# Retention and two gated layers on one core: decays on values and queries, a second pair of score banks, weight conversion in small steps

## The chip, the cores and the metric

The kernel runs on one core of a Trainium2 chip. The metric is the device time of one execution in microseconds (us). Before the change it is 634.4 us, the median of three runs (631.55 to 635.45).

## What is computed

The first stage is retention, a recurrence per batch and head with a fixed decay gamma of the head; after it come two gated layers on its output.

```python
gamma = 1.0 - 2.0 ** (-5.0 - np.arange(H))
for t in range(S):
    state = gamma * state + k[t] (outer) v[t]      # per batch and head, 64 x 64
    y[t] = (1 / sqrt(D)) * q[t] @ state
x = y as (1536 tokens, 512)
x = ((x @ w_a) * (x @ w_b)) @ w_out                # d_ff 1536
h = x @ w_in;  out = (h * sigmoid(1.702 * h)) @ w_out2   # d_ff 2048
```

There are 2 batches, 8 heads, 768 time steps and 64 columns per head. The weights arrive as 64-bit floats and are turned on the chip into a high and a low float32 part, and every product of a layer is made as three matmuls of such parts.

## The kernel before

Retention is done in chunks. The 1536 tokens are 12 blocks of 128 (`NBLK`), six to a batch (`SEQ`). In block n, with c = n % 6:

- `att_load` brings q and k transposed and k and v plain into one tile `raw`, of which there are four. Load n+4 stands on SP's queue behind the last reader of block n.
- `att_scores` makes k'q for the 8 heads in two banks of PSUM, and VectorE multiplies them by `mask`, which holds causality, scale and gamma^(t-s) of every head (L144, two instructions). There is one pair of these banks, so scores of block n+1 wait until block n's masks are through.
- `att_kd` (GpSimd, L118) puts decays on k; `att_kv` adds kd'v to a bank that runs over the six blocks, and VectorE writes the state, scaled by `gdec` (L168, L170).
- `att_qd` (GpSimd, L109) puts decays on q; `att_av` makes v'a and, where c > 0, adds state'qd. ScalarE copies the sum to `xh` (L200), VectorE writes the rest, `xl` (L64).

A weight piece of 128x512 goes through three steps, each one `w_point` behind the other: `w_carry` (ScalarE, L234 and L235), `w_round` (four VectorE instructions, L242 to L249), and `w_parts` (ScalarE writes `wh` at L255, then GpSimd writes `wl` at L64). In retention there is one `w_point` at the end of blocks 3, 5, 7, 9 and 11. In the layers w_points stand behind every set of matmuls.

The schedule is manual: each engine runs its instructions in the order in which the program writes them. The layers, `up` (L296) and `down` (L333), come after block 11. The first `up` uses piece 0, the second piece 1, and so on.

Of the kernel before, what the change touches and what calls it, by code (L numbers as in the profile page):

```python
# [39 lines left out]
def retention_moe_kernel(  # L40
# [25 lines left out]

    mask = attp.tile([P, 2, NP, P], F32, tag="mask", name="mask", bufs=1)
    decays = attp.tile([P, NP * P + H + NP, 1], F32, tag="decays", name="decays", bufs=1)  # L70
    kdec = attp.tile([P, SEQ - 1, H, 1], F32, tag="kdec", name="kdec", bufs=1)
    kinv = attp.tile([P, SEQ - 1, H, 1], F32, tag="kinv", name="kinv", bufs=1)
    gdec = attp.tile([P, SEQ - 2, NP, 1], F32, tag="gdec", name="gdec", bufs=1)
    dec = decays[:, 0:NP * P].rearrange("p (a t) o -> p a (t o)", t=P)
    kdec0, gdec0 = decays[:, NP * P:NP * P + H], decays[:, NP * P + H:]
    zero = attp.tile([P, P], F32, tag="zero", name="zero", bufs=1)
    x = [xp.tile([P, KD, NT], F32R, tag=t, name=t) for t in ("xh", "xl")]
    raw_t, qd_t, kd_t, a_t, state_t = {}, {}, {}, {}, {}
    kv_t = [None]

    def att_load(n):
        if n >= NBLK:
            return
        t = attp.tile([P, 4, DM], F32, tag="raw", name="raw", bufs=RAWBUFS)
        if n == 0:
            m = cmask.rearrange("p (c h t) -> p c h t", c=2, t=P)
            nc.sync.dma_start(out=t[:, 0, :], in_=att[n][:, 0, :])
            nc.scalar.dma_start(out=t[:, 1, :], in_=att[n][:, 1, :])
            for h2 in range(2):
                nc.scalar.dma_start(out=mask[:, h2], in_=m[:, h2])  # L90
            nc.sync.dma_start(out=t[:, 2:4, :], in_=att[n][:, 2:4, :])
            nc.scalar.dma_start(out=decays.rearrange("p a o -> p (a o)"), in_=cdec)
        else:
            for i in (0, 2):
                nc.sync.dma_start(out=t[:, i:i + 2, :], in_=att[n][:, i:i + 2, :])
        raw_t[n] = t

    def att_decays():

        for c in range(1, SEQ - 1):  # L100
            nc.gpsimd.tensor_tensor(out=kdec[:, c], in0=kdec0, in1=kinv[:, c], op=ALU.mult)
        nc.gpsimd.tensor_copy(gdec[:, 0], gdec0)
        for c in range(1, SEQ - 2):
            nc.gpsimd.tensor_tensor(out=gdec[:, c], in0=gdec[:, c - 1], in1=gdec0, op=ALU.mult)

    def att_qd(n):
        if n < NBLK and n % SEQ > 0:
            t = attp.tile([P, NP, P], F32, tag="qd", name="qd")
            nc.gpsimd.tensor_tensor(  # L109
                out=t, in0=raw_t[n][:, 0, :].rearrange("p (a t) -> p a t", t=P), in1=dec, op=ALU.mult  # L110
            )
            qd_t[n] = t

    def att_kd(n):
        c = n % SEQ
        if n < NBLK and c < SEQ - 1:
            t = attp.tile([P, H, D], F32, tag="kd", name="kd")
            nc.gpsimd.tensor_tensor(  # L118
                out=t,
                in0=raw_t[n][:, 2, :].rearrange("p (h d) -> p h d", d=D),  # L120
                in1=(kdec[:, c] if c else kdec0).to_broadcast([P, H, D]),
                op=ALU.mult,
            )
            kd_t[n] = t

    def att_scores(n):

        if n >= NBLK:
            return
        r = raw_t[n]  # L130
        ps = [ps_att.tile([P, NP, P], F32, tag="sc", name="ps_sc", bufs=2) for _ in range(2)]
        for p in range(NP):
            for h2 in range(2):
                rows = slice(64 * h2, 64 * h2 + 64)
                nc.tensor.matmul(  # L135
                    ps[h2][:, p, :],
                    r[rows, 1, p * P:(p + 1) * P],
                    r[rows, 0, p * P:(p + 1) * P],
                    start=True,
                    stop=True,  # L140
                )
        for h2 in range(2):
            a = attp.tile([P, NP, P], F32, tag="a", name="a", bufs=4)
            nc.vector.tensor_tensor(out=a, in0=ps[h2], in1=mask[:, h2], op=ALU.mult)  # L144
            a_t[n, h2] = a

    def att_kv(n):
        c = n % SEQ
        if c == SEQ - 1:
            return  # L150
        if c == 0:
            kv_t[0] = ps_att.tile([P, NP, D], F32, tag="kv", name="ps_kv")
        ps = kv_t[0]
# [12 lines left out]
        t = attp.tile([P, NP, D], F32, tag="state", name="state")
        if c == 0:
            nc.vector.tensor_copy(t, ps)  # L168
        else:
            nc.vector.tensor_tensor(out=t, in0=ps, in1=gdec[:, c - 1].to_broadcast([P, NP, D]), op=ALU.mult)  # L170
        state_t[n + 1] = t

    def att_av(n):
        c = n % SEQ
        ps = ps_att.tile([P, NP, P], F32, tag="av", name="ps_av", bufs=2)
        for p in range(NP):
            for h2 in range(2):
                h = 2 * p + h2
                nc.tensor.matmul(  # L179
                    ps[64 * h2:64 * h2 + 64, p, :],  # L180
                    raw_t[n][:, 3, h * D:(h + 1) * D],
                    a_t[n, h2][:, p, :],
                    start=(p == 0),
                    stop=(c == 0),
                    skip_group_check=True,
                )
        if c > 0:
            for p in range(NP):
                for h2 in range(2):
                    rows = slice(64 * h2, 64 * h2 + 64)  # L190
                    nc.tensor.matmul(  # L191
                        ps[rows, p, :],
                        state_t[n][rows, p, :],
                        qd_t[n][rows, p, :],
                        start=False,
                        stop=True,
                        skip_group_check=True,
                    )
        hi, lo = (t[:, :, n * P:(n + 1) * P] for t in x)
        nc.scalar.copy(hi, ps)  # L200
        lo_part(nc.vector, lo, ps, hi)

# [31 lines left out]
        nc.scalar.activation(out=wt[i], in_=high.bitcast(F32), func=ACTF.Abs)  # L234
        nc.scalar.activation(out=low, in_=low.bitcast(U32), func=ACTF.Copy, scale=2.0 ** -29)  # L235

    def w_round(i):
        src = wraw.pop(i)
        carry, high = src[:, :, 0], src[:, :, 1]
        t = wt[i]  # L240
        ti = t.bitcast(I32)
        nc.vector.tensor_scalar(out=t, in0=t, scalar1=F64_LOW, scalar2=F64_HIGH, op0=ALU.max, op1=ALU.min)  # L242
        nc.vector.tensor_scalar(  # L243
            out=ti, in0=ti, scalar1=3, scalar2=0x3FFFFFFF, op0=ALU.logical_shift_left, op1=ALU.bitwise_and
        )
# [12 lines left out]
    def w_point():  # L258
# [117 lines left out]
    def layer(ph):  # L376
        nfb = (C1 if ph == 1 else C2) // FB
        for fb in range(nfb):
# [25 lines left out]
            for q in range(4):  # L404
# [5 lines left out]
                flush(ps, ph, fb, q, fine)  # L410
                w_points(2)

    with tc.manual_schedule():
        nc.vector.memset(zero, 0.0)
        for n in range(2):
            att_load(n)
        gamma = [1.0 - 2.0 ** (-5.0 - h) for h in range(H)]
        for c in range(1, SEQ - 1):
            for h in range(H):
                nc.gpsimd.memset(kinv[:, c, h, :], gamma[h] ** (-float(P) * c))  # L420

        ps = ps_att.tile([P, NP, P], F32, tag="av", name="ps_warm", bufs=2)
        for _ in range(WARM):
            nc.tensor.matmul(ps[:, 0, :], zero, zero, start=True, stop=True)
        att_load(2)
        att_load(3)
        att_scores(0)
        att_kd(0)
        att_decays()
        for n in range(NBLK):  # L430
            if n == 0:
                att_kv(n)
                att_scores(n + 1)
            else:
                att_scores(n + 1)
                att_kv(n)
            att_kd(n + 1)
            att_av(n)
            att_qd(n + 1)
            att_load(n + RAWBUFS)  # L440
            if n in (1, 2, 3):
# [71 lines left out]
```

## Time and profile before

| quantity | value |
|---|---|
| median of 3 runs | 634.4 us |
| time of the profiled execution | 635.11 us |
| span of the profiled execution (first to last instruction) | 633.2 us |
| mean granted TensorE clock | 0.976 of full |
| TensorE, VectorE, ScalarE, GpSimd busy | 611.5, 381.9, 227.7, 143.6 us |

The span is 1.9 us shorter than the time of the same execution. Busy shares are means over two stages: retention, some 72 us, and the layers after it. Line numbers are those of the kernel before. PE is TensorE's matmuls, DVE is VectorE, ACT ScalarE, POOL GpSimd, SP the engine that issues most transfers.

### The profile page before, as it was taken

What the parts mean: (1) busy time and instruction counts of PE and PEld (TensorE: products, weight loads), DVE (VectorE), ACT (ScalarE), POOL (GpSimd) and SP (SyncE); (2) the same over time, 40 slices, a digit from 0 to 9 for tenths busy, and PEclk for the clock granted to TensorE, in tenths of its full rate; (3) what the DMA queues carried; (4) which work ended last, traced back from release to release, by engine and by line L of the source; (5) the groups of instructions that cost most, each with busy time, mean ns of one, the idle gap of its engine ahead of it and who ended that gap; (6) DMA issues with size and microseconds to landing.
All of it is one profiled execution on the core that took longest, in us unless ns stands there. A gap on an engine that the chain in (4) does not pass through costs nothing.

```text
span 633.2 us, 7760 instructions
## 1 busy us (share of the span) xinstructions
PE 611.5 (97%) x3174; PEld 508.3 (80%) x3174; DVE 381.9 (60%) x433; ACT 227.7 (36%) x310; POOL 143.6 (23%) x132
## 2 busy tenths in 40 slices
PE   5977899999999999999999999999999999999996
PEld 5866688888888888888888888888888888888885
DVE  1667747786026878226886758762779277936422
ACT  0212245445124453014554245643554055314300
POOL 3534223333002332002331302230223021302000
PEclk7977799999999999999999999999999999999999
DMA  8883123333012222111222211140023112200022
GB/s 315 277 330 128 48 85 101 100 99 100 0 35 67 92 86 90 33 34 47 87 101 67 67 33 42 58 134 33 34 68 119 49 33 67 66 1 0 1 99 100
DMA packets 15491, 52.67 MB, mean 83 GB/s; under 512 B 1632, under 2 KB 1632, under 8 KB 15456
## 3 DMA queue, kind: packets, MB, share of 16 engines
q1 hardware_dynamic: 14880, 51.12, 24.2%
q10 hardware_dynamic: 576, 1.05, 0.5%
q8 instruction: 25, 0.41, 0.2%
q14 instruction: 10, 0.08, 0.0%
HBM read 49.03 MB, written 3.15 MB: 82 GB/s over the span
## 4 chain that ended last, share of the span: by engine, by line
PE 93%; DVE 3%; DMA 2%; ACTq 0%; ACT 0%; POOL 0%; issue 0%; DVEq 0%; SPq 0%; POOLq 0%
PE ps L296 52%; PE ps L333 36%; PE ps_sc L135 2%; PE ps_av L179 2%; DMA decays<-in_cdec_dram 1%; PE ps_av L191 1%; DMA raw<-in_att_dram 1%; PE ps_kv L158 1%; DVE wt L246 1%; DVE wt L242 0%; DVE wt L249 0%; DVE wt L243 0%; DVE a L144 0%; DVE xl L64 0%; DVE part L350 0%; ACT xh L200 0%
## 5 line engine op out<-in xcount | busy, mean ns | idle before, releaser
L64 POOL TENSOR_TENSOR wl<-wt,wh 128x512 fp32r<-128x512 f32 x68 | 116.6, 1718 | 421.1 <-ACT wh L255 396.4
L296 PE MATMUL ps<-xh,wh 128*128 128x512 f32 x480 | 129.7, 391 | 0.0
L296 PE MATMUL ps<-xl,wh 128*128 128x512 f32 x480 | 128.8, 389 | 0.0
L296 PE MATMUL ps<-xh,wl 128*128 128x512 f32 x480 | 128.8, 389 | 0.0
L296 PEld LDWEIGHTS ps<-xh,wh 128*128 128x128 f32 x480 | 90.5, 189 | 19.1 <-issue 0.3
L296 PEld LDWEIGHTS ps<-xl,wh 128*128 128x128 f32 x480 | 90.2, 188 | 18.8
L296 PEld LDWEIGHTS ps<-xh,wl 128*128 128x128 f32 x480 | 90.1, 188 | 18.7
L242 DVE TENSOR_SCALAR wt<-wt 128x512 f32<-128x512 f32 x68 | 67.0, 986 | 55.6 <-ACT wt L234 55.6
L313 ACT CAST gh<-sb 128x1536 fp32r<-128x1536 f32 (+1 forms) x42 | 44.2, 1051 | 111.6 <-DVE sb L312 111.6
L64 DVE TENSOR_TENSOR gl<-sb,gh 128x1536 fp32r<-128x1536 f32 (+1 forms) x42 | 51.5, 1226 | 46.9 <-ACT gh L313 46.9
L312 DVE TENSOR_TENSOR sb<-ps,sb 128x1536 f32<-128x1536 f32 (+1 forms) x42 | 51.3, 1220 | 46.8 <-ACT sb L396 24.4
L350 DVE TENSOR_TENSOR part<-ps,part 128x1536 f32<-128x1536 f32 (+1 forms) x24 | 35.5, 1487 | 48.1 <-PE ps L333 48.1
L246 DVE SCALAR_TENSOR_TENSOR wt<-wraw,wt 128x512 int32<-128x512 int32 x68 | 58.7, 863 | 2.3
L255 ACT CAST wh<-wt 128x512 fp32r<-128x512 f32 x68 | 41.9, 617 | 39.7 <-DVE wt L249 39.7
L333 PE MATMUL ps<-wh,gh 128*128 128x512 f32 x192 | 55.2, 389 | 0.0
L333 PE MATMUL ps<-wl,gh 128*128 128x512 f32 x192 | 55.2, 389 | 0.0
L333 PE MATMUL ps<-wh,gl 128*128 128x512 f32 x192 | 55.2, 389 | 0.0
L249 DVE CUSTOM_DVE_ANT_0 wt<-wraw,wt 128x1024 uint16<-128x1024 uint16 x68 | 50.4, 742 | 6.4
L234 ACT ACTIVATE wt<-wraw 128x512 f32<-128x512 f32 x68 | 45.7, 673 | 2.5 <-POOL wl L64 1.4
L235 ACT ACTIVATE wraw<-wraw 128x512 int32<-128x512 uint32 x68 | 45.2, 664 | 0.0
L396 ACT ACTIVATE sb<-ps 128x1536 f32<-128x1536 f32 (+1 forms) x24 | 23.8, 1029 | 54.0 <-PE ps L296 54.0
L243 DVE TENSOR_SCALAR wt<-wt 128x512 int32<-128x512 int32 x68 | 41.3, 607 | 2.3
(42 smaller groups left out, 530.9 us busy)
## 6 DMA issues: line engine op xcount, KB each, us to landing
wraw<-in_w_dram SPq DMA_DIRECT2D x68, 512.0 KB, 3.6
raw<-in_att_dram SPq DMA_DIRECT2D x23, 512.0 KB, 7.6
out_dram<-part SPq DMA_DIRECT2D x3, 768.0 KB, 3.5
out_dram<-part SPq DMA_DIRECT2D x3, 256.0 KB, 2.1
mask<-in_cmask_dram ACTq DMA_DIRECT2D x2, 256.0 KB, 6.9
decays<-in_cdec_dram ACTq DMA_DIRECT2D x1, 262.0 KB, 9.1
raw<-in_att_dram ACTq DMA_DIRECT2D x1, 256.0 KB, 4.5
raw<-in_att_dram SPq DMA_DIRECT2D x1, 256.0 KB, 4.0
```

The source lines that it names most:

```text
L64: engine.tensor_tensor(out=lo, in0=src, in1=hi.bitcast(F32), op=ALU.subtract)
L234: nc.scalar.activation(out=wt[i], in_=high.bitcast(F32), func=ACTF.Abs)
L235: nc.scalar.activation(out=low, in_=low.bitcast(U32), func=ACTF.Copy, scale=2.0 ** -29)
L242: nc.vector.tensor_scalar(out=t, in0=t, scalar1=F64_LOW, scalar2=F64_HIGH, op0=ALU.max, op1=ALU.min)
L243: nc.vector.tensor_scalar(out=ti, in0=ti, scalar1=3, scalar2=0x3FFFFFFF, op0=ALU.logical_shift_left, op1=ALU.bitwise_and)
L246: nc.vector.scalar_tensor_tensor(out=ti, in0=high, scalar=-0x40000000, in1=ti, op0=ALU.bitwise_and, op1=ALU.bitwise_or)
L249: nc.vector.tensor_tensor(out=ti, in0=ti, in1=carry, op=ALU.add)
L255: nc.scalar.copy(hi, t)
L296: nc.tensor.matmul(ps[:, g, :], l, r, start=(i == 0 and k == 0), stop=(i == 2 and k == max(late or now)), skip_group_check=True,)
L312: nc.vector.tensor_tensor(out=sb[:, c], in0=ps[:, c], in1=sb[:, c], op=ALU.mult)
L313: nc.scalar.copy(gh[:, c], sb[:, c])
L333: nc.tensor.matmul(ps[:, n, :], l, r, start=(f == min(g_t) and i == 0), stop=(f == max(g_t) and i == 2), skip_group_check=True,)
```

## The change

The decays leave the masks, the keys and the state. Values are multiplied by a decay that grows backwards over the whole sequence (`vdec`, one column per head and chunk, `att_v`), queries by its inverse with the scale (`qdec`, `att_q`), so that one 128x128 mask of zeros and ones (`causal`) serves all heads, and the state is copied unscaled, by ScalarE. Scores now need the multiplied q (block 0 uses the raw one and scales its result instead). Block n's scores lie in a pair of banks of their own for odd n and in the layers' idle banks for even n, and one VectorE instruction masks all of them. `qdec` of chunk 1 is loaded; ScalarE makes that of the other chunks, four instructions each, in blocks 0 to 3. Loads are paired otherwise: q with v, plain k with transposed k.

The first three weight pieces are converted in steps over the blocks: carry at the end of block 1, 4, 7, and in the blocks that follow bits, sign and add; with add come the two parts and the next transfer. The layers begin with an empty conversion pipeline and piece 3 as the next.

```diff
+    def att_constants():
+        gamma = [1.0 - 2.0 ** (-5.0 - h) for h in range(H)]
+        for c in range(1, SEQ):
+            for h in range(H):
+                nc.gpsimd.memset(vinv[:, c, h, :], gamma[h] ** (-float(P) * c))
+        for c in range(SEQ):
+            for h in range(H):
+                rows = slice(64 * (h % 2), 64 * (h % 2) + 64)
+                nc.gpsimd.memset(gdec[rows, c, h // 2:h // 2 + 1], gamma[h] ** (float(P) * (c - 1)))
+    def att_qdec(c):
+        if c < SEQ and c != 1:
+            for p in range(NP):
+                nc.scalar.activation(
+                    out=qdec[:, c, p], in_=qdec[:, 1, p], func=ACTF.Copy, scale=gdec[:, c, p:p + 1]
+                )
+    def att_q(n):
+        if n < NBLK:
+            t = attp.tile([P, NP, P], F32, tag="q", name="q", bufs=3)
+            (nc.vector if n == 1 else nc.gpsimd).tensor_tensor(
+                out=t, in0=qv_t[n][:, 0, :].rearrange("p (a t) -> p a t", t=P), in1=qdec[:, n % SEQ], op=ALU.mult
             )
...
     def att_scores(n):
-        ps = [ps_att.tile([P, NP, P], F32, tag="sc", name="ps_sc", bufs=2) for _ in range(2)]
+        if n % 2:
+            ps = ps_att.tile([P, 2, G], F32, tag="sc", name="ps_sc")
+        else:
+            ps = ps_a.tile([P, NG, G], F32, tag="set", name="ps_sc")
...
-        for h2 in range(2):
-            a = attp.tile([P, NP, P], F32, tag="a", name="a", bufs=4)
-            nc.vector.tensor_tensor(out=a, in0=ps[h2], in1=mask[:, h2], op=ALU.mult)
-            a_t[n, h2] = a
+        a = attp.tile([P, 2 * NP, P], F32, tag="a", name="a")
+        nc.vector.tensor_tensor(
+            out=a,
+            in0=ps[:, 0:2, :].rearrange("p c (a t) -> p (c a) t", t=P),
+            in1=causal.to_broadcast([P, 2 * NP, P]),
+            op=ALU.mult,
+        )
...
-        if c == 0:
-            nc.vector.tensor_copy(t, ps)
-        else:
-            nc.vector.tensor_tensor(out=t, in0=ps, in1=gdec[:, c - 1].to_broadcast([P, NP, D]), op=ALU.mult)
+        nc.scalar.copy(t, ps)
...
+    def w_early(n):
+        i, k = divmod(n - 2, 3)
+        if i < 0 or i >= EARLY:
+            return
+        (w_bits, w_sign, w_add)[k](i)
+        if k == 2:
+            w_dma()
+            w_parts(i)
+            room[is_down[i]] -= 1
+            nxt["split"] += 1
...
     with tc.manual_schedule():
...
+        for n in range(RAWBUFS):
+            att_load(n)
         ps = ps_att.tile([P, NP, P], F32, tag="av", name="ps_warm", bufs=2)
+        warm(ps, WARM)
+        att_v(0)
+        att_vdec()
         att_scores(0)
+        att_q(1)
+        warm(ps, 8)
         for n in range(NBLK):
+            if n > 0:
+                att_scores(n + 1)
+            att_v(n + 1)
+            att_kv(n)
+            if n < SEQ:
+                att_qdec(n + 2 if n else 0)
+                if n == 0:
+                    att_qdec(2)
+            w_early(n)
+            att_av(n)
             if n == 0:
+                att_scores(1)
+            att_q(n + 2)
+            if n + RAWBUFS < NBLK:
+                att_load(n + RAWBUFS)
+            if n in (0, 1, 2, 9):
                 w_dma()
+            if n % 3 == 1 and n // 3 < EARLY:
+                w_carry(n // 3)
```

Of `w_round`, `w_bits` is L242 and L243, `w_sign` is L246, `w_add` is L249. For block 0 the transfers are q and v on SP's queue and k, `causal`, `vdec`, plain k and `qdec` on ScalarE's.

## Rows read from the trace of the kernel before

**Rows 1.** The page, part 1: busy time and share of each engine.
```profile
PE 611.5 (97%) x3174; PEld 508.3 (80%) x3174; DVE 381.9 (60%) x433; ACT 227.7 (36%) x310; POOL 143.6 (23%) x132
```
**Rows 2.** The chain that ended last, in order of time: start, length, what.
```profile
2.13 9.13 DMA decays<-in_cdec_dram
...
12.50 1.12 PE ps_kv L158 x16
...
24.28 1.09 PE ps_sc L135 x16
25.37 0.61 PE ps_kv L158 x16
25.98 0.88 PE ps_av L179 x16
26.86 1.02 PE ps_av L191 x16
...
40.56 2.67 PE ps_sc L135 x16
...
67.78 2.56 PE ps_av L179 x16
...
72.25 66.29 PE ps L296 x288
...
171.18 65.28 PE ps L296 x288
```
**Rows 3.** Waits of PE: total, times, longest.
```profile
PE ps_sc L135 <- DVE a L144: 7.2, 2, 4.2
...
PE ps_av L179 <- DVE a L144: 2.7, 1, 2.7
```
**Rows 4.** Stretches around two waits: busy of each engine, granted clock, DMA share, GB/s.
```profile
37.00:40.40 3.40, 0.55 (x11) 0.30 (x6) 3.33 (x4) 0.59 (x1) 2.02 (x3) 0.91 1.03 410
...
45.50:46.50 1.00, 1.00 (x12) 0.67 (x10) 0.00 (x0) 0.00 (x0) 0.00 (x0) 0.50 0.01 4
...
65.00:67.80 2.80, 0.09 (x3) 0.02 (x1) 2.73 (x5) 0.59 (x1) 0.39 (x1) 0.87 0.00 0
```
**Rows 5.** Timeline: start, length, engine, line, what, count, idle before.
```profile
37.55 1.63 DVE L246 SCALAR_TENSOR_TENSOR wt<-wraw,wt 128x512 int32<-128x512 int32 x1
...
39.21 0.69 DVE L249 CUSTOM_DVE_ANT_0 wt<-wraw,wt 128x1024 uint16<-128x1024 uint16 x1
39.82 1.28 DVE L144 TENSOR_TENSOR a<-ps_sc,mask 128x512 f32<-128x512 f32 x2
...
41.01 1.27 POOL L109 TENSOR_TENSOR qd<-raw,decays 128x512 f32<-128x512 f32 x1
...
47.85 0.62 ACT L255 CAST wh<-wt 128x512 fp32r<-128x512 f32 x1
...
48.55 1.29 POOL L64 TENSOR_TENSOR wl<-wt,wh 128x512 fp32r<-128x512 f32 x1 [6.26 <-ACT wh L255]
...
49.79 1.23 POOL L118 TENSOR_TENSOR kd<-raw,kdec 128x512 f32<-128x512 f32 x1
...
81.45 1.44 ACT L390 COPY sb<-ps 128x1536 f32<-128x1536 f32 x1 [6.91 <-PE ps L296]
...
93.48 2.35 POOL L64 TENSOR_TENSOR wl<-wt,wh 128x512 fp32r<-128x512 f32 x1 [6.80 <-ACT wh L255]
```
**Rows 6.** Groups by line and shape, 0 to 73 us: busy, mean ns, idle before.
```profile
L200 ACT CAST xh<-ps_av 128x512 fp32r<-128x512 f32 x12 | 7.0, 586 | 54.5 <-PE ps_av L191 40.9 <-PE ps_av L179 13.7
...
L234 ACT ACTIVATE wt<-wraw 128x512 f32<-128x512 f32 x4 | 2.8, 692 | 1.2 <-DMA wraw<-in_w_dram 1.2
...
L420 POOL MEMSET kinv<- 128x1 f32 x32 | 1.1, 98 | 0.3 <-POOLq L503 0.3
```
**Rows 7.** Stretches of the start: columns as in rows 4.
```profile
0.00:6.00 6.00, 4.95 (x24) 4.83 (x26) 0.17 (x1) 1.28 (x1) 1.32 (x36) 1.00 0.62 202
6.00:12.00 6.00, 1.04 (x16) 0.84 (x16) 1.38 (x2) 0.00 (x0) 0.60 (x1) 0.75 1.03 403
```

More of the change, by code (lines that the diff above doesn't have):

```diff
@@ L32 @@
 WARM = 11
+EARLY = 3
 F64_LOW = 2.0 ** -15
@@ L64, in lo_part @@
         engine.tensor_tensor(out=lo, in0=src, in1=hi.bitcast(F32), op=ALU.subtract)
[L69 to L75, printed above, removed]
+    causal = attp.tile([P, 1, P], F32, tag="causal", name="causal", bufs=1)
+    vdec = attp.tile([P, SEQ, H, 1], F32, tag="vdec", name="vdec", bufs=1)
+    vinv = attp.tile([P, SEQ, H, 1], F32, tag="vinv", name="vinv", bufs=1)
+    gdec = attp.tile([P, SEQ, NP], F32, tag="gdec", name="gdec", bufs=1)
+    qdec = attp.tile([P, SEQ, NP, P], F32, tag="qdec", name="qdec", bufs=1)
     zero = attp.tile([P, P], F32, tag="zero", name="zero", bufs=1)
     x = [xp.tile([P, KD, NT], F32R, tag=t, name=t) for t in ("xh", "xl")]
-    raw_t, qd_t, kd_t, a_t, state_t = {}, {}, {}, {}, {}
+    qv_t, kk_t, q_t, v_t, a_t, state_t = {}, {}, {}, {}, {}, {}
     kv_t = [None]
@@ L83, in att_load @@
             return
-        t = attp.tile([P, 4, DM], F32, tag="raw", name="raw", bufs=RAWBUFS)
+        qv, kk = (attp.tile([P, 2, DM], F32, tag=t, name=t, bufs=RAWBUFS) for t in ("qv", "kk"))
         if n == 0:
-            m = cmask.rearrange("p (c h t) -> p c h t", c=2, t=P)
-            nc.sync.dma_start(out=t[:, 0, :], in_=att[n][:, 0, :])
-            nc.scalar.dma_start(out=t[:, 1, :], in_=att[n][:, 1, :])
-            for h2 in range(2):
-                nc.scalar.dma_start(out=mask[:, h2], in_=m[:, h2])
-            nc.sync.dma_start(out=t[:, 2:4, :], in_=att[n][:, 2:4, :])
-            nc.scalar.dma_start(out=decays.rearrange("p a o -> p (a o)"), in_=cdec)
-        else:
-            for i in (0, 2):
-                nc.sync.dma_start(out=t[:, i:i + 2, :], in_=att[n][:, i:i + 2, :])
@@ L96, in att_load @@
[L96 to L110, printed above, removed]
-            )
-            qd_t[n] = t
@@ L114, in att_kd @@
[L114 to L117, printed above, removed]
+            nc.sync.dma_start(out=qv[:, 0, :], in_=att[n][:, 0, :])
+            nc.scalar.dma_start(out=kk[:, 0, :], in_=att[n][:, 1, :])
+            nc.scalar.dma_start(out=causal[:, 0, :], in_=cmask[:, 0:P])
+            nc.scalar.dma_start(
+                out=vdec[:, 0].rearrange("p h o -> p (h o)"), in_=cdec[:, NP * P:NP * P + H]
+            )
+            nc.sync.dma_start(out=qv[:, 1, :], in_=att[n][:, 3, :])
@@ new lines, in att_load @@
+            nc.scalar.dma_start(out=kk[:, 1, :], in_=att[n][:, 2, :])
+            nc.scalar.dma_start(out=qdec[:, 1].rearrange("p a t -> p (a t)"), in_=cdec[:, 0:NP * P])
+        else:
+            nc.sync.dma_start(out=qv, in_=att[n][:, 0:4:3, :])
+            nc.sync.dma_start(out=kk, in_=att[n][:, 1:3, :])
+        qv_t[n], kk_t[n] = qv, kk
+    def att_constants():
[7 more added lines that the diff above has]
+                nc.gpsimd.memset(gdec[rows, c, h // 2:h // 2 + 1], gamma[h] ** (float(P) * (c - 1)))
@@ new lines, in att_vdec @@
+    def att_vdec():
+        nc.vector.tensor_scalar(
+            out=causal, in0=causal, scalar1=0.0, scalar2=1.0, op0=ALU.is_gt, op1=ALU.mult
+        )
+        for c in range(1, SEQ):
+            nc.gpsimd.tensor_tensor(out=vdec[:, c], in0=vdec[:, 0], in1=vinv[:, c], op=ALU.mult)
+    def att_qdec(c):
[3 more added lines that the diff above has]
+                    out=qdec[:, c, p], in_=qdec[:, 1, p], func=ACTF.Copy, scale=gdec[:, c, p:p + 1]
+                )
@@ L118, in att_kd, with att_v @@
+    def att_q(n):
[3 more added lines that the diff above has]
+                out=t, in0=qv_t[n][:, 0, :].rearrange("p (a t) -> p a t", t=P), in1=qdec[:, n % SEQ], op=ALU.mult
+            )
+            q_t[n] = t
+    def att_v(n):
+        if n < NBLK:
+            t = attp.tile([P, H, D], F32, tag="v", name="v")
             nc.gpsimd.tensor_tensor(
                 out=t,
-                in0=raw_t[n][:, 2, :].rearrange("p (h d) -> p h d", d=D),
@@ L121, in att_kd @@
-                in1=(kdec[:, c] if c else kdec0).to_broadcast([P, H, D]),
+                in0=qv_t[n][:, 1, :].rearrange("p (h d) -> p h d", d=D),
+                in1=vdec[:, n % SEQ].to_broadcast([P, H, D]),
                 op=ALU.mult,
             )
-            kd_t[n] = t
+            v_t[n] = t
     def att_scores(n):
@@ L129, in att_scores @@
             return
-        r = raw_t[n]
-        ps = [ps_att.tile([P, NP, P], F32, tag="sc", name="ps_sc", bufs=2) for _ in range(2)]
+        if n % 2:
+            ps = ps_att.tile([P, 2, G], F32, tag="sc", name="ps_sc")
+        else:
+            ps = ps_a.tile([P, NG, G], F32, tag="set", name="ps_sc")
+        q = qv_t[n][:, 0, :].rearrange("p (a t) -> p a t", t=P) if n == 0 else q_t[n]
         for p in range(NP):
@@ L135, in att_scores @@
                 nc.tensor.matmul(
-                    ps[h2][:, p, :],
-                    r[rows, 1, p * P:(p + 1) * P],
-                    r[rows, 0, p * P:(p + 1) * P],
+                    ps[:, h2, p * P:(p + 1) * P],
+                    kk_t[n][rows, 0, p * P:(p + 1) * P],
+                    q[rows, p, :],
                     start=True,
@@ L141, in att_scores @@
                 )
-        for h2 in range(2):
-            a = attp.tile([P, NP, P], F32, tag="a", name="a", bufs=4)
-            nc.vector.tensor_tensor(out=a, in0=ps[h2], in1=mask[:, h2], op=ALU.mult)
-            a_t[n, h2] = a
+        a = attp.tile([P, 2 * NP, P], F32, tag="a", name="a")
[4 more added lines that the diff above has]
+            op=ALU.mult,
+        )
+        a_t[n] = a
     def att_kv(n):
@@ L159, in att_kv @@
                     ps[64 * h2:64 * h2 + 64, p, :],
-                    kd_t[n][:, h, :],
-                    raw_t[n][:, 3, h * D:(h + 1) * D],
+                    kk_t[n][:, 1, h * D:(h + 1) * D],
+                    v_t[n][:, h, :],
                     start=(c == 0 and p == 0),
@@ L180, in att_av @@
                     ps[64 * h2:64 * h2 + 64, p, :],
-                    raw_t[n][:, 3, h * D:(h + 1) * D],
-                    a_t[n, h2][:, p, :],
+                    v_t[n][:, h, :],
+                    a_t[n][:, NP * h2 + p, :],
                     start=(p == 0),
@@ L193, in att_av @@
                         state_t[n][rows, p, :],
-                        qd_t[n][rows, p, :],
+                        q_t[n][rows, p, :],
                         start=False,
@@ L199, in att_av @@
         hi, lo = (t[:, :, n * P:(n + 1) * P] for t in x)
+        if n == 0:
+            t = attp.tile([P, NP, P], F32, tag="q", name="x0", bufs=3)
+            nc.vector.tensor_tensor(out=t, in0=ps, in1=qdec[:, 0], op=ALU.mult)
+            ps = t
         nc.scalar.copy(hi, ps)
@@ L235, in w_carry, with w_bits @@
         nc.scalar.activation(out=low, in_=low.bitcast(U32), func=ACTF.Copy, scale=2.0 ** -29)
-    def w_round(i):
-        src = wraw.pop(i)
-        carry, high = src[:, :, 0], src[:, :, 1]
+    def w_bits(i):
         t = wt[i]
@@ L245, in w_round, with w_sign, w_add @@
         )
+    def w_sign(i):
+        ti = wt[i].bitcast(I32)
         nc.vector.scalar_tensor_tensor(
-            out=ti, in0=high, scalar=-0x40000000, in1=ti, op0=ALU.bitwise_and, op1=ALU.bitwise_or
+            out=ti, in0=wraw[i][:, :, 1], scalar=-0x40000000, in1=ti, op0=ALU.bitwise_and, op1=ALU.bitwise_or
         )
-        nc.vector.tensor_tensor(out=ti, in0=ti, in1=carry, op=ALU.add)
+    def w_add(i):
+        ti = wt[i].bitcast(I32)
+        nc.vector.tensor_tensor(out=ti, in0=ti, in1=wraw.pop(i)[:, :, 0], op=ALU.add)
     def w_parts(i):
@@ L262, in w_point @@
         if stage[1] is not None:
-            w_round(stage[1])
+            for step in (w_bits, w_sign, w_add):
+                step(stage[1])
             w_dma()
@@ L411, in layer, with warm @@
                 w_points(2)
+    def warm(ps, n):
+        for _ in range(n):
+            nc.tensor.matmul(ps[:, 0, :], zero, zero, start=True, stop=True)
     with tc.manual_schedule():
         nc.vector.memset(zero, 0.0)
-        for n in range(2):
+        att_constants()
+        for n in range(RAWBUFS):
             att_load(n)
[L417 to L420, printed above, removed]
         ps = ps_att.tile([P, NP, P], F32, tag="av", name="ps_warm", bufs=2)
[L423 to L426, printed above, removed]
+        warm(ps, WARM)
+        att_v(0)
+        att_vdec()
         att_scores(0)
-        att_kd(0)
-        att_decays()
+        att_q(1)
+        warm(ps, 8)
         for n in range(NBLK):
-            if n == 0:
[L432 to L441, printed above, removed]
+            if n > 0:
[4 more added lines that the diff above has]
+                att_qdec(n + 2 if n else 0)
+                if n == 0:
+                    att_qdec(2)
+            w_early(n)
+            att_av(n)
+            if n == 0:
+                att_scores(1)
[3 more added lines that the diff above has]
+            if n in (0, 1, 2, 9):
                 w_dma()
-            if n >= 3 and n % 2:
-                w_point()
+            if n % 3 == 1 and n // 3 < EARLY:
+                w_carry(n // 3)
         layer(1)
```

## The prediction

> **What bounds the kernel now.** I read the busy shares first: TensorE is busy for 97% of the span [rows 1], so time can only come from its gaps, its clock and work taken from it. The chain in order of time says where. From 72.25 us on it is matmuls of the layers without a gap, at one pace: 288 of them take 65.28 us at full clock, and the first 288 take 66.29 [rows 2]. The change leaves these matmuls as they are, so what it can alter is the stage before, 0 to 72.2 us, and that extra 1.0 us. The layers and the end take 633.2 - 72.2 = 561.0 us.
>
> In retention a block with all its parts costs TensorE 1.09 (scores) + 0.61 (kv) + 0.88 (av) + 1.02 (state) = 3.60 us at full clock, back to back [rows 2]. Blocks 0 and 6 have no state part, 5 and 11 no kv, so twelve are about 40 us. The stage takes 72, and the rest is in three places:
> - The start. The first kv waits until 12.5 us for the decays, which land 9.13 us after their issue [rows 2].
> - Masks behind conversion steps. TensorE waits 7.2 us in two cases and 2.7 in a third for a mask [rows 3]. The four VectorE steps of a weight piece stand ahead of it in VectorE's queue: the sign step took 1.63 us beside a GpSimd pass, then the add 0.69, then the masks 1.28 [rows 5].
> - The clock after each. It had begun to fall within the waits (a mean of 0.91 over 37.0 to 40.4, 0.87 over 65.0 to 67.8) and was 0.50, the lower of its two levels, up to 46.5 [rows 4]; eight-head scores take 2.67 instead of 1.09 then [rows 2]. From 40.56 to 46.5 that is 5.9 us at half speed, 2.95 lost per wait. The third wait is where the 1.0 us at the layers' start comes from.
>
> **Part by part.**
> *Work that gets lighter.* VectorE loses the second mask instruction's fixed cost (one of 1024 columns, at most the 1.28 us of the two [rows 5]) and the state. Its block is then 1.3 + 0.7 for xl (one pass as the add [rows 5]) + one conversion step of at most 1.63 [rows 5] = 3.6 us: it just fits into TensorE's block, and masks are due only a block later because scores have two pairs of banks. So the three old waits go, and I cost VectorE at nothing; if it lags, a block of slack covers it.
>
> *The start.* ScalarE's transfers are smaller: up to `qdec` they carry 256 + 64 + 4 + 256 + 256 KB, 0.84 MB, where those up to the decays carried 1.03. Up to 6 us 202 GB/s moved, 1.21 MB, and 403 after [rows 7], so the decays landed when 3.3 MB were through, ScalarE's share being 0.31. By this share `qdec` needs 2.7 MB: 6 + 1.5/0.403 = 9.7 us. With equal shares it is 7.2; I take 9.7, which rests on the same two queues.
>
> One rule speaks against these small transfers. The Trainium skill, DMA: Bandwidth & Descriptors, section Bandwidth, gives 0.68 us for 4 KB and 0.95 us for 64 KB, in transfers issued from GpSimd; `vdec` and `causal` are of these sizes, and at 403 GB/s they are 0.17. By the page, as an estimate, `qdec` would land 1.46 us later, and the sum below would be 628.6 instead of 627.1; no row here shows a transfer so small.
>
> *A new chain in blocks 1 to 5.* Scores now need q x qdec. ScalarE makes a chunk's `qdec` behind the state copy of block n in its queue, GpSimd makes q(n+2) from it, and scores(n+2) wait. One turn: scores 1.09 and kv 0.61 [rows 2]; handover and state copy 0.1 + 0.38; four `qdec`; q 1.27 [rows 5]; three handovers of 0.05. The price per column of ScalarE is (1.44 - 0.59)/1024 us from the 1536- and 512-column copies [rows 5, 6], so 256 columns are 0.38 and 128 are 0.27 from PSUM; from SBUF 512 columns are 0.69 [rows 6], so 128 are 0.37. Four take 1.1 to 1.5; I take 1.2, as instructions on one engine overlap a little. The turn is 4.8 us against the 3.60 of TensorE's work: 1.2 us idle in each. From `qdec` at 9.7, eight copies 2.4, q(2) 1.27 and 0.15 give scores(2) at 13.5; then scores(3) at 18.3, scores(4) at 23.1, scores(5) at 27.9. Old blocks ran at 3.6, so the change gives back part of its own start here.
>
> The first carry stands on ScalarE ahead of block 2's state copy and waits for weight piece 0, which comes behind five loads: 6.1 MB by 6 + 4.9/0.403 = 18.1 us. Two passes of 0.69 [rows 6] end at 19.5, before kv(2) ends at 20.0: nothing, and one for one if it lands later. GpSimd's 88 memsets instead of 32 at 1.1 us together [rows 6] are 3.1 us ahead of v(0), while the transfers come; at 98 ns each they would be 8.6, which is still before `qdec`. v passes (1.23 [rows 5]) lie beside TensorE's work, as GpSimd's v and q make 2.5 us a block.
>
> *A new wait at blocks 4 and 7.* In `w_early` the step add is followed by `w_parts`, so GpSimd's queue holds v(n+1), wl, q(n+2). q(n+2) is behind wl, which waits for wh, which waits for add, which is behind the mask of block n+1. The same standing still is in the trace: GpSimd idled 6.26 us for wh at 47.85, wl ran at 48.55, and kd only at 49.79 [rows 5]; kd was not due then, but q will be. From the start of scores(n+1): scores end 1.16, mask to 2.45, add 0.69 to 3.1, wh 0.62 to 3.8, wl 1.29 to 5.15, q 1.27 to 6.45 [rows 5], scores(n+2) at 6.5 where TensorE is done at 3.6. Idle 2.9 us, for n = 4 (scores(6)) and n = 7 (scores(9)); at n = 7 the mask is behind xl and it is 0.1 later. At n = 10 no q follows. As the 2.7 us wait was followed by half clock [rows 3, 4], I count 2.95 more for each. Bounds: without the fall it is 2.9 per wait; with gaps hidden by something late, nothing.
>
> *The sum.* Scores(6) 27.9 + 6.5 = 34.4. Block 5 (no kv, 2.99 at full, all at half) to 40.35; block 6 (2.6) to 42.95; block 7 with its wait (6.6) to 49.55; block 8 (3.6 + 2.95) to 56.1; blocks 9 and 10 to 63.3; block 11 (1.9) to 65.2. The layers start at 65.2 instead of 72.2 and at full clock: 65.2 + 561.0 - 1.0 = 625.2 us of span, with the 1.9 us around it 627.1 against 635.11. The median of the runs is 634.4, 0.9989 of that: **626.4 us**, 1.3% faster.
>
> *The layers.* Their conversion pipeline begins empty. Before, the wl of the w_point behind the second `up` ended at 93.48 + 2.35 [rows 5], 23.6 us after the layers' start. In the new order that one makes piece 3, which the fourth `up` needs 3 x 8.2 + 1.8 = 26.3 us after it (an `up` is 36 of the 288 matmuls [rows 2]; wl is its ninth). It is hidden with 2.7 us to spare, and later pieces have one `up` more.
>
> **The rivals.**
> 1. The clock holds through both waits: for it, they are little longer than 2.7 us; against it, both stretches in which it fell had begun to fall before the wait was over [rows 4]. 65.2 - 5.9 gives 621.2 in the profile, 620.5. If something else in these blocks is late anyway, so that the waits themselves are covered, another 5.8 go: 614.7.
> 2. The clock falls in the early blocks already: each turn has 1.2 us or more idle, a length that no row of before shows either way. A turn is then 2 x 1.70 + 3.1 = 6.5 instead of 4.8. Three turns and slower scores(5), 1.1: 6.2 us more, 633.3 in the profile, 632.6. The gain is nearly gone.
> 3. Slower: the empty pipeline. If ScalarE's or VectorE's queue at the layers' start runs over 2.7 us later than in the rows above, the fourth and fifth `up` each wait for their weights. Two waits of 2.7 with 2.95 of half clock each are 11.3 us: 638.4, 637.7 on the median. Against it: the queues hold fewer conversion steps there than before.
> 4. The change does not do what it says, masks still wait for conversion. Two of the three waits would come back, with their clock: 627.1 + 2 x 6 = 639; only if VectorE runs a whole block late.
>
> **How the numbers follow.** Forecast 0.58 (623.5 to 629.5: `qdec` from 7.2 to 11 us, the four copies at 1.1 to 1.5); rival 1 0.17, of which 0.05 for 614.7; rival 2 0.16; rival 3 0.05; rival 4 0.02; 0.02 for others. The range of 619.5 to 633 takes in rival 2 and the first form of rival 1. A measurement of this kernel tells 1% from no change, which is 628.1 here: three quarters of the forecast's chance and rival 1 are below it, 0.61; rival 2, most of the rest and part of 4 lie within 1%, 0.33; slower by over 1% (640.7) is 0.06 with worse forms of rivals 3 and 4.
>
> **What would show it.** Layers start near 65 us. GpSimd idles on wh twice, with q right behind wl; scores(6) and scores(9) wait for q some 2.9 us, and score matmuls after them run at clock 0.50. Scores(2) to scores(5) stand about 4.8 us apart and wait for GpSimd. No wait for a mask on TensorE, and none in the layers. I am wrong if GpSimd's wl does not hold q up, if a wait in the early blocks is long enough for the clock, or if a weight piece comes late in the layers.

## The result, and the profile after

The changed kernel takes 626.15 us (median of 4 runs, 625.21 to 627.93) against 634.35 (4 runs of the kernel before); the ratio is 0.9881, 95% interval 0.9842 to 0.9919. Runs of the kernel before, on all chips used here, fall into two groups, 630.5 to 632 us (mean granted clock 0.986 to 0.989) and 634 to 636.4 us (0.976 to 0.981); its trace is of the second, and against the first the gain is some 5 us. The forecast was 626.4. The profiled execution took 626.12 us with a span of 624.3, where 627.1 and 625.2 had been worked out. Line numbers below are those of the kernel that the rows come from; in the changed one L159 is the scores, L167 the mask, L130 q, L138 v, L123 the query decays, L195 the state copy, L65 every low part, L342 and L379 the layers.

The page's part 1, and the chain that ended last (start, length, what), answer to [rows 1, 2]:

```profile
PE 607.0 (97%) x3190; PEld 504.9 (81%) x3190; DVE 371.7 (60%) x414; ACT 237.1 (38%) x340; POOL 150.0 (24%) x187
```
```profile
14.71 1.44 PE ps_sc L159 x16
...
36.15 2.08 PE ps_sc L159 x16
...
49.78 2.08 PE ps_sc L159 x16
...
64.16 65.51 PE ps L342 x288
...
162.31 65.28 PE ps L342 x288
```

The layers start at 64.16 us instead of 72.25, and their first 288 matmuls take 65.51 instead of 66.29. That is 8.1 + 0.8 = 8.9 us, the whole difference of the spans (633.2 to 624.3); the rest of the layers is as it was. Waits of TensorE, then of GpSimd up to 72 us (total, times, longest):

```profile
PE ps_sc L159 <- POOL q L130: 10.2, 6, 2.8
PE ps_warm L462 <- DVE zero L465: 1.1, 1, 1.1
PE ps_kv L186 <- POOL v L138: 1.1, 1, 1.1
```
```profile
POOL q L130 <- ACT qdec L123: 9.2, 4, 2.8
POOL wl L65 <- ACT wh L288: 8.7, 3, 3.4
```

The 9.9 us of waits for masks [rows 3] are gone. In their place stand 10.2 us of waits for q: four of them because q waits for its decays, two because wl is ahead of it. Of the other waits, that of the first kv has become short: 1.1 us where the kernel before has 5.5. From the trace before, this wait, the start of scores(2), and two of the stretches at the lower clock (columns as in [rows 4]):

```profile
PE ps_kv L158 <- POOL kd L118: 5.5, 1, 5.5
```
```profile
16.72 1.44 PE L135 MATMUL ps_sc<-raw 64*128 64x128 f32 x16
```
```profile
55.00:60.30 5.30, 5.22 (x48) 4.70 (x48) 3.27 (x7) 0.00 (x0) 0.55 (x1) 0.50 0.36 102
67.70:74.00 6.30, 6.22 (x37) 4.92 (x38) 2.64 (x6) 1.70 (x4) 0.52 (x1) 0.51 0.30 86
```

Without the wait ahead of the warm-up, TensorE's waits fall from 15.7 us (masks 9.9, kd 5.5, a transfer 0.3) to 11.3, which is half of the 8.9 us. The other half lies with the clock: three stretches at the lower level, of 3.2 to 3.4 us, instead of four of 3.5 to some 6 us. The earlier start does not last. Scores(2) come 2.0 us earlier (14.71 against 16.72), but scores(4) 0.7 us later (25.02 against 24.28 [rows 2]) and scores(8) 2.8 us later (43.34 against 40.56); the gain comes in the last four blocks, where the kernel before still has two waits for masks and three stretches at half clock. Around the first of the two wl waits the timeline shows the order that was forecast (start, length, engine, line, what):

```profile
32.19 0.68 DVE L282 CUSTOM_DVE_ANT_0 wt<-wraw,wt 128x1024 uint16<-128x1024 uint16 x1
...
32.90 0.62 ACT L288 CAST wh<-wt 128x512 fp32r<-128x512 f32 x1 [0.81 <-DVE wt L282]
...
33.60 1.27 POOL L65 TENSOR_TENSOR wl<-wt,wh 128x512 fp32r<-128x512 f32 x1 [2.81 <-ACT wh L288]
...
34.83 1.27 POOL L130 TENSOR_TENSOR q<-qv,qdec 128x512 f32<-128x512 f32 x1
...
36.15 2.08 PE L159 MATMUL ps_sc<-q,kk 64*128 64x128 f32 x16 [2.64 <-POOL q L130]
```

Add, wh, wl, q, scores: each starts within 0.1 us of the end of the one before. GpSimd stood for 2.81 us at wl with nothing between it and q. The clock after this wait and after the second one, by stretch (PE, PEld, DVE, ACT and POOL busy, granted clock, DMA share, GB/s), to set beside [rows 4]:

```profile
36.15:38.20 2.05, 2.05 (x18) 1.83 (x18) 0.00 (x0) 0.00 (x0) 2.05 (x2) 0.50 0.84 282
38.20:39.20 1.00, 1.00 (x12) 1.00 (x12) 0.93 (x1) 0.00 (x0) 0.12 (x1) 0.50 0.72 229
39.20:40.20 1.00, 1.00 (x18) 0.83 (x16) 0.97 (x3) 0.00 (x0) 0.23 (x1) 0.93 0.94 328
...
49.78:51.80 2.02, 2.02 (x18) 1.79 (x18) 0.00 (x0) 0.00 (x0) 2.02 (x2) 0.50 0.88 358
51.80:52.80 1.00, 1.00 (x20) 1.00 (x20) 0.89 (x1) 0.00 (x0) 0.16 (x1) 0.50 0.10 41
52.80:53.80 1.00, 1.00 (x19) 0.85 (x16) 0.97 (x3) 0.37 (x1) 0.00 (x0) 0.90 0.00 0
```

### The profile page after: what moved, and what is told of

The parts are those of the page before. It is cut to its first block, busy times and chain, and to the rows that moved or that the text cites. A ratio compares the mean times of both kernels' runs of the same rounds, so it can differ in the third digit from the quotient of the medians.

```text
span 624.3 us, 7868 instructions
## 1 busy us (share of the span) xinstructions
PE 607.0 (97%) x3190; PEld 504.9 (81%) x3190; DVE 371.7 (60%) x414; ACT 237.1 (38%) x340; POOL 150.0 (24%) x187
## 4 chain that ended last, share of the span: by engine, by line
PE 93%; POOL 3%; issue 3%; DVE 0%; DVEq 0%; POOLq 0%
PE ps L342 52%; PE ps L379 37%; PE ps_sc L159 1%; PE ps_av L204 1%; PE ps_av L216 1%; POOL v L138 1%; POOL q L130 1%; POOL gdec L109 1%; PE ps_kv L186 1%; POOL vinv L105 0%; DVE part L396 0%; POOL vdec L117 0%; DVEq L560 0%; POOL wl L65 0%; POOLq L138 0%
## 5 line engine op out<-in xcount | busy, mean ns | idle before, releaser
L65 POOL TENSOR_TENSOR wl<-wt,wh 128x512 fp32r<-128x512 f32 x68 | 117.0, 1725 | 410.1 <-ACT wh L288 385.1
L342 PE MATMUL ps<-xh,wh 128*128 128x512 f32 x480 | 128.9, 389 | 0.0
L342 PE MATMUL ps<-xl,wh 128*128 128x512 f32 x480 | 128.8, 389 | 0.0
L342 PE MATMUL ps<-xh,wl 128*128 128x512 f32 x480 | 128.8, 389 | 0.0
L342 PEld LDWEIGHTS ps<-xl,wh 128*128 128x128 f32 x480 | 90.1, 188 | 18.7
L342 PEld LDWEIGHTS ps<-xh,wh 128*128 128x128 f32 x480 | 90.0, 188 | 18.8 <-issue 0.2
L342 PEld LDWEIGHTS ps<-xh,wl 128*128 128x128 f32 x480 | 90.1, 188 | 18.7
L269 DVE TENSOR_SCALAR wt<-wt 128x512 f32<-128x512 f32 x68 | 63.8, 938 | 53.5 <-ACT wt L263 53.5
L65 DVE TENSOR_TENSOR gl<-sb,gh 128x1536 fp32r<-128x1536 f32 (+1 forms) x42 | 51.5, 1226 | 47.1 <-ACT gh L359 47.1
L276 DVE SCALAR_TENSOR_TENSOR wt<-wraw,wt 128x512 int32<-128x512 int32 x68 | 55.7, 819 | 2.2
L379 PE MATMUL ps<-wl,gh 128*128 128x512 f32 x192 | 55.2, 389 | 0.0
L379 PE MATMUL ps<-wh,gh 128*128 128x512 f32 x192 | 55.2, 389 | 0.0
L379 PE MATMUL ps<-wh,gl 128*128 128x512 f32 x192 | 55.2, 389 | 0.0
L436 ACT COPY sb<-ps 128x1536 f32<-128x1536 f32 x12 | 17.4, 1446 | 66.6 <-PE ps L342 66.6
```

The lines of the kernel that those rows point to most:

```text
L65: engine.tensor_tensor(out=lo, in0=src, in1=hi.bitcast(F32), op=ALU.subtract)
L276: nc.vector.scalar_tensor_tensor(out=ti, in0=wraw[i][:, :, 1], scalar=-0x40000000, in1=ti, op0=ALU.bitwise_and, op1=ALU.bitwise_or)
L342: nc.tensor.matmul(ps[:, g, :], l, r, start=(i == 0 and k == 0), stop=(i == 2 and k == max(late or now)), skip_group_check=True,)
L379: nc.tensor.matmul(ps[:, n, :], l, r, start=(f == min(g_t) and i == 0), stop=(f == max(g_t) and i == 2), skip_group_check=True,)
```

## The experiments

All kernels are compared with runs of the kernel before on the same chip. Each edit below is against the changed kernel, except where it says otherwise.

**1. Parts behind q.** `w_parts` is moved out of `w_early`:

```diff
             att_q(n + 2)
+            w_early_parts(n)      # wh and wl of the piece whose add is in this block
```

> The changed kernel with one thing moved: the two parts of an early weight piece (wh on ScalarE, wl on GpSimd) are issued behind q(n+2) instead of ahead of it. Theory (GpSimd's order makes the two waits): the waits of 2.64 and 2.77 us before scores(6) and scores(9) go, and the half clock after them (3.2 us at half each, 1.6 lost); the layers start at 64.1 - 5.4 - 3.2 = 55.5 us and the span falls from 624.3 to about 615.7. Rival (add on VectorE or the loads hold scores up as well): waits of 1 to 2 us stay at these blocks and the span stays above 620.

Measured: 621.23 us, ratio 0.9809 [0.9762, 0.9857]; span 619.5, layers from 59.4. The waits before scores(6) and (9) are gone, and the clock is 0.999 over the span, but of the 8.6 us expected 4.8 came:

```profile
33.47 0.59 ACT L229 CAST xh<-ps_av 128x512 fp32r<-128x512 f32 x1 [1.47 <-PE ps_av L216]
33.96 0.62 ACT L288 CAST wh<-wt 128x512 fp32r<-128x512 f32 x1
...
34.66 1.29 POOL L65 TENSOR_TENSOR wl<-wt,wh 128x512 fp32r<-128x512 f32 x1 [2.72 <-ACT wh L288]
...
35.90 1.25 POOL L138 TENSOR_TENSOR v<-qv,vdec 128x512 f32<-128x512 f32 x1
...
37.11 1.44 POOL L130 TENSOR_TENSOR q<-qv,qdec 128x512 f32<-128x512 f32 x1
...
38.61 1.16 PE L159 MATMUL ps_sc<-q,kk 64*128 64x128 f32 x16 [2.04 <-POOL q L130]
```

wh now stands behind xh on ScalarE, so it comes later, GpSimd stands at wl again, and the next block's v and q wait in its place: 2.04 us before scores(7), 1.57 before scores(10). The theory holds for the two waits and the clock; that nothing would take their place was wrong: the wait moved one block on.

**2. Query decays ahead of the state copy.** In block n, `att_qdec(n + 2)` is put ahead of the scores of n+1.

> The changed kernel with the query decays of chunk n+2 made by ScalarE ahead of block n's state copy instead of behind it. Theory (the chain scores, kv, state copy, decays, q, scores sets the pace of the early blocks): the waits of 0.26, 1.15 and 1.15 us before scores(3), (4) and (5) go, blocks 2 to 4 run at 3.6 us each, the layers start 2.6 us earlier, at 61.5; the waits before scores(2), (6) and (9) stay. Rival (GpSimd's v and q or the loads set the pace): scores(3) to (5) stay 4.8 us apart.

One run: 624.42 us, span 622.6, layers from 62.5. Scores(3) follow scores(2) after 3.73 us without a wait: the chain was right. But scores(4) wait longer than before:

```profile
20.64 0.69 ACT L263 ACTIVATE wt<-wraw 128x512 f32<-128x512 f32 x1 [1.53 <-DMA wraw<-in_w_dram]
```
```profile
24.46 2.08 PE L159 MATMUL ps_sc<-q,kk 64*128 64x128 f32 x16 [2.38 <-POOL q L130]
```

ScalarE stands at the first carry until the weight piece lands at 20.6, and the decays of chunk 4 are behind it. Of the 2.6 us expected, 1.7 came by the span, but most of that is not the move's. Scores(5) start at 29.45 instead of 29.84, 0.4 us earlier, and scores(6) at 35.89 instead of 36.15. Then block 5 took 3.13 us instead of 4.61, as the clock held behind a wait of 2.76 us that is no shorter (columns as above):

```profile
35.89:37.00 1.11, 1.11 (x18) 0.99 (x18) 0.00 (x0) 0.00 (x0) 1.11 (x2) 1.00 0.96 334
...
48.04:49.00 0.96, 0.96 (x8) 0.96 (x10) 0.00 (x0) 0.00 (x0) 0.96 (x2) 0.50 1.02 418
```

Behind the next wait, before scores(9), it was 0.50. With one execution, how often the clock holds here is not known.

**3. Small memsets on VectorE.** `nc.vector.memset(gdec[...])` instead of `nc.gpsimd.memset`.

> The changed kernel with the 48 small memsets of gdec on VectorE instead of GpSimd. Theory (their 6.6 us hold v(0) up, then kv(0), the state copy and the decays behind it on ScalarE): v(0) starts at about 6.3 instead of 8.77, kv(0) right behind the warm-ups at 8.8, scores(2) at about 13.6 instead of 14.71, the layers about 1 us earlier, at 63. Rival (the transfer of qdec, landed at 9.1, sets the start anyway): less than 0.5 us.

One run: 626.01 us, span 624.2.

```profile
0.94 4.80 DVE L109 MEMSET gdec<- 64x1 f32 x48
...
7.26 1.04 POOL L138 TENSOR_TENSOR v<-qv,vdec 128x512 f32<-128x512 f32 x1 [5.15 <-DMA vdec<-in_cdec_dram]
...
14.16 1.16 PE L159 MATMUL ps_sc<-q,kk 64*128 64x128 f32 x16 [2.19 <-POOL q L130]
```
```profile
20.58 0.70 ACT L263 ACTIVATE wt<-wraw 128x512 f32<-128x512 f32 x1 [1.98 <-DMA wraw<-in_w_dram]
...
24.67 1.16 PE L159 MATMUL ps_sc<-q,kk 64*128 64x128 f32 x16 [2.08 <-POOL q L130]
```

v(0) is 1.5 us earlier and scores(2) 0.55, scores(3) 1.26. By scores(4) all but 0.35 us has been given back to the same transfer: the first carry waits 1.98 us for it. The layers start at 64.07, 0.1 us earlier: the rival's number, but not its reason, as `qdec` had landed. Neither theory had this; a faster start only waits longer at the first weight piece.

**4. All three moves.**

> The three moves of the runs before in one kernel. Theory: their gains add, as they are at different blocks: 8.6 + 2.6 + 1.0 = 12.2 us, the layers start at about 52 and the span is about 612, 1.9% under the changed kernel and 3.1% under the kernel before. Rival (once one wait is gone the next engine is late): less than two thirds of it, above 616.

Measured: 621.85 us, 0.9815 [0.9778, 0.9851], span 620.8: 3.5 us of the 12.2 expected, and no better than the first move alone. The theory that the gains add falls, and the rival holds. TensorE waits 2.12 us before scores(2), 3.39 before scores(4) (the transfer, 2.58 us on ScalarE), 2.04 before (7) and 1.57 before (10); behind the second and the third the clock fell to 0.50.

**5 and 6. One part of the change alone.** The kernel before with the small steps, and the changed kernel with the w_points of before:

```diff
 # 5: kernel before
+            w_early(n)
             att_av(n)
...
-            if n >= 3 and n % 2:
-                w_point()
+            if n % 3 == 1 and n // 3 < EARLY:
+                w_carry(n // 3)
 # 6: changed kernel, EARLY = 0
-            if n % 3 == 1 and n // 3 < EARLY:
-                w_carry(n // 3)
+            if n >= 3 and n % 2:
+                w_point()
```

> One part of the change alone: the kernel before (masks with decays, decays on keys and state, one pair of score banks), with the weight pieces converted in small steps over the blocks at the places of the changed kernel. Theory (the time of before went into masks behind four steps in a row, and nothing in the new form of retention is needed against that): the 9.9 us of waits for masks go and with them three stretches of half clock; wl is ahead of qd here too, but qd is due only at the state part, 2.5 us later than scores, so it costs under 1 us; the layers start at 56 to 59 us instead of 72.2 and the time is 617 to 621, less than the changed kernel's. Rival (VectorE's single pair of banks is too tight even for one step a block): waits for masks of 1 us or more in most blocks, time 624 to 632.

> One part of the change undone: the changed kernel with the conversion of before, whole w_points at the end of blocks 3, 5, 7, 9 and 11. Theory (the second pair of banks gives masks a block of slack, so four steps in a row are hidden, and wl comes two blocks behind its add, so that it does not stand waiting ahead of q): no wait before scores(6) and (9), masks late by at most 1 us, the layers start at 55 to 58 us, span 616 to 619. Rival (the spreading is what frees the masks): waits for masks of 2 to 4 us at two or three blocks with half clock, span 624 or more.

Measured: the steps alone 623.5 us, 0.9849 [0.981, 0.9889]; the new retention alone 626.41 us, 0.9905 [0.9873, 0.9937]. Waits of TensorE, first of the former, then of the latter:

```profile
PE ps_av L192 <- POOL qd L110: 3.9, 3, 2.1
PE ps_sc L136 <- DVE a L145: 1.4, 1, 1.4
```
```profile
PE ps_sc L159 <- POOL q L130: 7.0, 5, 2.2
PE ps_av L204 <- DVE a L167: 5.7, 3, 3.1
```

Each part alone brings about what the whole brings (0.9881), the steps alone by the medians 2.7 us more, on another chip; the gains do not add. Both fell short of their theories: 623.5 us where 617 to 621 were expected, and a span of 624.5 us where 616 to 619 were. With the steps alone, waits for masks fall from 9.9 to 1.4 us, so the theory is right there, but wl ahead of qd costs 3.9, not under 1 us, and the layers still begin at half clock (67.10 us for the first 288 matmuls). With the new retention alone, no wait stands before scores(6) and (9), as the theory had it, but the second pair of banks does not hide four steps in a row: TensorE waits 1.24, 1.35 and 3.11 us for masks. The time is the rival's; of its two or three waits of 2 to 4 us with half clock only the last came, and the clock fell after it.

**7 and 8. wl one block later.** wh stays behind the add; wl is issued behind the next block's q. Run 8 also has the memsets on VectorE, the decays of chunks 3 to 5 ahead of the state copies of blocks 1 and 2, and carry, steps and add one block later, so that the first carry is no longer ahead of those decays.

```diff
             nc.scalar.copy(hi, t)
-            lo_part(nc.gpsimd, lo, t, hi)
+            held.append((n, lo, t, hi))
...
             att_q(n + 2)
+            w_late(n)        # lo_part of the piece held since the block before
```

> The changed kernel with wh made at its old place behind the add (so that ScalarE has it early) and wl one block later, behind that block's q. Theory (in the run with both parts behind q, GpSimd stood at wl again, waiting for a wh that was behind xh on ScalarE, with the next v and q behind it: waits of 2.04 and 1.57 us before scores(7) and (10)): with wh already there when GpSimd comes to wl, these go too, the layers start at about 55.7 us and the span is about 616. Rival (GpSimd is simply full in these blocks): waits of 1 us or more stay, span above 618.

> The run before, with gdec's memsets on VectorE, the query decays of chunks 3, 4 and 5 ahead of the state copies of blocks 1 and 2, and the first carry (and with it all early steps) one block later, as it made ScalarE wait for the weight piece's transfer ahead of the decays of chunk 4. Theory: the chain that paced blocks 2 to 5 and the 3.4 us wait before scores(4) go, blocks follow at 3.6 us from scores(2) at 13.5 on, the layers start at 50 to 51 us, span 610 to 612. Rival (the loads are the next limit: 15.5 MB before the last block's at 400 GB/s need about 42 us): waits for transfers, layers at 53 to 56, span 613 to 616.

Measured: run 7 617.43 us, 0.9758 [0.972, 0.9796], span 615.8, layers from 55.6; run 8 612.81 us, 0.9685 [0.9648, 0.9722], span 610.9. Waits of TensorE in run 7, then in run 8, and the layers' start in run 8:

```profile
PE ps_sc L159 <- POOL q L130: 4.7, 4, 2.2
```
```profile
PE ps_sc L159 <- POOL q L130: 2.3, 2, 2.2
```
```profile
50.73 65.50 PE ps L352 x288
```

Both came out as expected. Run 7's four waits stand before scores(2) to (5), none behind a wl. In run 8 one wait of 2.2 us before scores(2) and one of 0.15 are left; the loads did not become the limit. Run 8 beats both kernels; how its 4.6 us over run 7 divide among its three moves was not tried.

**9. The kernel before with both.** Small steps, and wl one block later behind qd.

> The kernel before with spread steps (masks, keys and state as before) and wl one block later, behind that block's qd. Theory (the gain is that of the conversion steps, not of the new form of retention): the 3.9 us of waits for qd go and the half clock at the layers' start with them (1.8 us), the layers start at about 56, span about 616, the same as the changed kernel with wl late. Rival (the old form's start and single pair of banks cost more): 2 us or more above that run.

Measured: 619.88 us, 0.9795 [0.9751, 0.984], span 618.9, layers from 58.7. No wait for qd is left. It is 2.45 us over run 7 on the same chip, so the rival holds: with the steps at these places the new form of retention is worth some 2 to 3 us. They are not lost at the old start: kv(0) stands at 12.47, at half clock, against 9.90 in run 7, but scores(5) at 29.36 against 29.78. They are lost from there on, where the carry waits for its transfer, VectorE's steps, with the masks behind them, wait for the carry, and the clock falls in that block. First this run, then scores(5) and (6) of run 7:

```profile
26.24 0.69 ACT L235 ACTIVATE wt<-wraw 128x512 f32<-128x512 f32 x1 [4.80 <-DMA wraw<-in_w_dram]
...
29.36 2.28 PE L136 MATMUL ps_sc<-raw 64*128 64x128 f32 x16 [1.35 <-DVE a L145]
...
35.14 1.16 PE L136 MATMUL ps_sc<-raw 64*128 64x128 f32 x16
```
```profile
29.78 1.16 PE L159 MATMUL ps_sc<-q,kk 64*128 64x128 f32 x16 [1.15 <-POOL q L130]
...
33.38 1.16 PE L159 MATMUL ps_sc<-q,kk 64*128 64x128 f32 x16
```

Whether a carry one block later, as in run 8, would close this gap for the old form was not tried.

## Why the prediction was right, and where it was not

The time was right to 0.3 us and the mechanism as forecast; some terms were off, and that their errors cancelled so closely is luck: the four runs alone lie 2.7 us apart. Starts of the scores of a block, from the timelines, and of the layers from the chain:

| start of | forecast us | measured us |
|---|---|---|
| scores(2) | 13.5 | 14.71 |
| scores(3), (4), (5) | 18.3, 23.1, 27.9 | 20.19, 25.02, 29.84 |
| scores(6) | 34.4 | 36.15 |
| scores(7), (8), (9) | 40.35, 42.95, 49.55 | 40.76, 43.34, 49.78 |
| scores(10) | 56.1 | 54.84 |
| layers | 65.2 | 64.16 |

- *Waits for masks go*: right. No mask is left among TensorE's waits, and run 6 shows that the small steps are needed for that in the new form.
- *The start*: 1.2 us too early. Rows of GpSimd show why:

```profile
0.74 1.43 POOL L105 MEMSET vinv<- 128x1 f32 x40 [0.29 <-POOLq L554]
...
2.06 6.63 POOL L109 MEMSET gdec<- 64x1 f32 x48
8.77 1.04 POOL L138 TENSOR_TENSOR v<-qv,vdec 128x512 f32<-128x512 f32 x1
```

  The term that failed is the 3.1 us for 88 memsets (3.0 by its own working): 40 went 36 ns apart, near the 34 of before, but the 48 on 64 partitions 138 ns apart. The prediction's bound of 8.6 us was near the truth, and it was called harmless since `qdec` lands later; but the chain of v(0), kv(0) and the state copy stands ahead of the query decays on ScalarE, and the sum did not count it. With these memsets on VectorE scores(2) start at 13.52 and 13.53 in runs 4 and 8, as forecast, and at 14.16 in run 3, where the scores of block 0 started late. `qdec` itself was there at 9.07, near the 9.7 worked out from the queues' shares. The 1.46 us more that the estimate by the Trainium skill, DMA: Bandwidth & Descriptors, section Bandwidth, put on the two small transfers would have made it 11.2. That did not come, but by 9.07 us ScalarE's queue had 0.86 of 2.31 MB, a share of 0.37 and not 0.31, so that a smaller price of small transfers is not excluded.
- *The chain of 4.8 us*: right at full clock, 25.02 - 20.19 = 4.83 and 29.84 - 25.02 = 4.82; run 2 shows that it was this chain. The first turn took 5.48, as its matmuls ran at half clock behind a wait of 2.19. That is rival 2, for one turn, and by the prediction's own sign (a wait in the early blocks long enough for the clock) it was wrong there. In these blocks the change gave back not a part of its start, but more than all of it.
- *The first weight piece*: forecast at 18.1, it lands at 20.5 to 20.6 (runs 2 to 4). In the changed kernel the late start covered it; with a better start it is the next wait.
- *wl ahead of q*: right in place and length, 2.64 and 2.77 us where 2.9 and 3.0 were forecast; runs 1 and 7 confirm it by moving it.
- *Half clock after them*: the fall was right, the price not. It lasted 3.2 us and not 5.9, so it cost about 1.6 each instead of 2.95; why it was shorter than in the kernel before stays open. Blocks 5 and 8 took 4.61 and 5.06 us instead of 5.95 and 6.55, 2.8 us less together, which paid for the late start (1.75 us at scores(6)).
- *The layers*: right. Piece 3's wl ended 22.9 us after the layers' start (forecast 23.6, needed at 26.3), and TensorE has no wait in the layers:

```profile
84.74 2.35 POOL L65 TENSOR_TENSOR wl<-wt,wh 128x512 fp32r<-128x512 f32 x1 [21.14 <-ACT wh L288]
```

What stays open: how the 2 to 3 us of the new form divide between the free state and mask work on VectorE, the second pair of banks and the wait for the weight piece was not tried part by part.

## What to carry to other kernels

In a kernel whose engines run in program order, follow each queue past the instruction that is moved: an operation that waits (wl, the first carry, the state copy) delays everything behind it, and what it delays may be due much sooner than itself. When a step is cut into small pieces, the waiting piece should be issued when its input is known to be there, not when its predecessor is issued: moving the early wl by a block was worth as much here as the whole change. Two cures for the same wait do not add, and a faster start is worth only as much as the next transfer allows.

## What the runs showed of the hardware

- GpSimd's memsets of one column: 36 ns apart on 128 partitions, 138 ns on 64 partitions (alternating halves); VectorE took 100 ns for the latter (4.80 us for 48). What makes it slow, the number of partitions or the alternation, was not tried.
- A wait of TensorE of 2.2 us before scores(2), at the same work, was followed by half clock in two traces (the changed kernel and run 7) and by full clock in five (runs 1, 2, 3, 6 and 8). The granted clock of that stretch (the third number from the right) in the changed kernel, then in run 2, with waits of 2.19 and 2.20 us:

```profile
14.70:16.00 1.30, 1.29 (x16) 1.15 (x16) 1.30 (x2) 0.00 (x0) 1.30 (x1) 0.79 1.02 389
```
```profile
14.60:16.00 1.40, 1.32 (x23) 1.20 (x24) 1.40 (x2) 0.37 (x2) 1.40 (x2) 1.00 1.02 388
```

  Nor did the length of the wait alone tell: in run 2 two waits of 2.76 us were followed by 1.00 and by 0.50 (above), and in run 4 a wait of 3.39 us was followed by full clock for the first 0.7 us of work and by 0.50 from 1.7 us after its end at the latest. Stretches at half clock after a wait lasted from 3.2 us (the changed kernel, before scores(7)) to some 6 us (the kernel before, from 67.7 us on) of work.
